# Decode attention and gated MLP with gradients on one core: layer norm on another engine, weight loads one turn earlier, a third PSUM pair at the end, a bf16 softmax shift

## The chip, the core and the metric

The kernel runs on one core of a Trainium2 chip. A core has five engines that run their own instruction streams, each in order: PE (TensorE, matrix products; its weight loads are listed apart as PEld), DVE (VectorE), ACT (ScalarE), POOL (GpSimd) and SP (SyncE). They work out of SBUF (128 partitions), PE writes into PSUM (8 banks of 128 x 512 fp32), and 16 DMA engines move data between SBUF and HBM. In this kernel SP issues nearly all loads and POOL nearly all stores. The metric is the device time of one execution in microseconds, the median over runs. Lower is better.

## What is computed

A forward pass and all its gradients, for batch 2 and a single query position, with bf16 data:

```python
xn = layernorm(x)                                   # x: 2 x 1 x 576
q  = xn @ wq                                        # 32 heads of 128
k, v = caches of 16 heads x 4096 x 128, each for 2 query heads
p  = softmax(q . k * 128 ** -0.5)
A  = (p . v) @ wo
B  = ((xn @ w_gate) * (xn @ w_up)) @ w_down         # 576 -> 4608 -> 576
out = x + A + B
# outputs: out, and for a given grad_out the gradients of
# x, k_cache, v_cache, wq, wo, w_gate, w_up, w_down
```

The caches are 2 x 16 x 4096 x 128 (33.6 MB each) and are read once; their gradients, as large, are written once. With the weights and their gradients 92.5 MB are read and 92.5 MB written.

## The kernel before, in words

**Attention.** The main loop has 16 steps (`NIT`): four groups of four KV heads, two batch rows, two halves of two heads. A step loads two K heads and two V heads, 1 MB each (`head_load`). `slot` handles one head: in two halves, `head_scores` transposes 128 x 1024 elements on DVE (`t32`, into `X`) and multiplies them on PE into a PSUM tile of the tag "sc" (two buffers). After the two K heads comes `softmax`: the maximum per partition (`mx`), a PE transpose to one row (`mT`), a maximum over the row (`m4`), its repetition (`mr`), a one-row product that spreads it over the partitions (`nb_ps`), then the exponential on ACT and the sums. All of this up to the exponential is fp32. After the V heads come `dscores` and `end_of_V`; `end_of_K` of a step follows early in the next step. Each of these two contains a `contract` of 64 matmuls over the heads' tiles, after which the tiles' buffers are free. Loads of heads and weights share one tag of 12 buffers, "nat", so a load is issued on SP only when an earlier tile is done with.

**Gradients of the caches.** They are outer products of one row with another. `outer_units` returns eight units for each step and cache: a unit makes 8 matmuls into a PSUM pair (`ps_o`, 128 x 2 x 512 fp32, two buffers), and `evac` copies it to SBUF as bf16, on DVE or ACT, whichever has the smaller running load (`load["v"]`, `load["s"]`). Four units fill 1 MB, which POOL then stores. The SBUF staging tiles of all stores share a tag, "st", of five buffers.

**Side work.** The MLP is cut in nine slices of 512 columns. `mlp_units` gives eight lists of functions for a slice: `loads` (wgu, wd: 1.77 MB), then `gate_up` and `down`, `grads` and `back`, and five lists of outer products with evictions. `back_units` gives nine lists for a finished group of heads: `first` (the output product with wo, the transposes `R`, and the stationaries `Wm` on DVE and `Wt` on POOL), `second` (the gradient of the norm through `dxn`), then the gradients of wo (`outer_o`, staged in `sto`) and wq (`outer_q`, `outer_qt`, staged in `stq` and `stqt`). The lists wait in `side`. In every slot, `more(2)` issues two units of cache gradients after each half, and then `other(per)` issues the next `per` lists, where `per` is a quarter of what is waiting. A new slice is added when fewer than five lists wait.

**The end.** After the loop: `end_of_K`, the K gradients of the last step, the last group's `back_units`, mixed with `final_units` (`prepare`, `output`: the forward result; `rows`: a product over `accx` on PE that gathers the gradient of the norm; `gradient`: nine small DVE steps over 2 x 576 elements and a store).

**The start.** The layer norm is eight DVE instructions over 2 x 576 elements with one square root on ACT (lines 168 to 188). POOL meanwhile clears the tiles `Wdy`, `W` (two), `dM` and others. DVE then prepares small constant tiles from the identity matrix, the last being `sel2`.

**Order.** A scheduler lays out each engine's instructions by priority and by its own estimates, and each engine then runs its stream strictly in that order, waiting on semaphores. `Block` keeps a unit's matmuls together.

Of the kernel before, what the change touches and what calls it, by code (L numbers as in the profile page):

```python
# [23 lines left out]
def kernel(  # L24
# [57 lines left out]

    class Block:
# [20 lines left out]
    def evac(out, in_, cols):  # L104
        cv = 0.16 + cols * 0.00104
        cs = 0.19 + cols * 0.00083
        if load["v"] + cv < load["s"] + cs:
            load["v"] += cv
            nc.vector.tensor_copy(out=out, in_=in_)  # L109
        else:  # L110
            load["s"] += cs
            nc.scalar.copy(out, in_)  # L112

# [43 lines left out]
    for be in range(4):  # L157
        nc.vector.tensor_copy(sel[:, be], view(ident[:], 0, P, 64 * (be // 2) + be % 2, [[0, 4], [2, 32]]))
        nc.vector.tensor_copy(selA[:, be], view(ident[:], 0, P, 32 * be, [[0, 4], [1, 32]]))
    one1 = const.tile([1, 1], FP32, name="one1")  # L160
# [7 lines left out]
    nc.vector.tensor_copy(x_f[:], x_bf[:])  # L168

    mu = const.tile([2, 1], FP32, name="mu")  # L170
    nc.vector.reduce_sum(mu[:], x_f[:], axis=AX.X)
    nc.vector.tensor_scalar(mu[:], mu[:], 1.0 / D, None, op0=ALU.mult)
    xn_f = sb.tile([2, D], FP32, tag="nat", bufs=12, name="xn_f")
    nc.vector.tensor_scalar(xn_f[:], x_f[:], mu[:], None, op0=ALU.subtract)
    xsq = sb.tile([2, D], FP32, tag="X", bufs=3, name="xsq")
    var = const.tile([2, 1], FP32, name="var")
    nc.vector.tensor_tensor_reduce(
        out=xsq[:], in0=xn_f[:], in1=xn_f[:], scale=1.0 / D, scalar=0.0,
        op0=ALU.mult, op1=ALU.add, accum_out=var[:],
    )  # L180
# [3 lines left out]
    nc.scalar.activation(rstd[:], var[:], AF.Sqrt, bias=eps_t[:], scale=1.0)  # L184
    nc.vector.reciprocal(rstd[:], rstd[:])
    nc.vector.tensor_scalar(xn_f[:], xn_f[:], rstd[:], None, op0=ALU.mult)
    xn_bf = sb.tile([2, D], BF16, tag="st", bufs=5, name="xn_bf")
    nc.vector.tensor_copy(xn_bf[:], xn_f[:])
# [27 lines left out]
    nc.gpsimd.memset(Wdy[:], 0.0)  # L216
# [8 lines left out]
    for t in range(2):  # L225
        nc.gpsimd.memset(W[t][:], 0.0)
    nc.gpsimd.memset(dM[:], 0.0)
# [340 lines left out]
    def outer_units(rows, bd, b, l0, oview):  # L568
        m = {}

        def unit(x, ch, A):
            def f():
                if ch == 0 and A == 0:
                    m["st"] = stile([P, 4, 8, Dh], "so")
                st = m["st"]
                o = ps_o()
                with Block() as mm:
                    for c in range(4):
                        for aa in range(2):
                            a = 2 * A + aa  # L580
                            mm(o[:, aa, c * Dh:(c + 1) * Dh], lhsT=rows[32 * a:32 * a + 32, 4 * ch + c, :],
                                             rhs=bd[32 * a:32 * a + 32, x * Dh:(x + 1) * Dh], start=True, stop=True)
                evac(st[:, 2 * A:2 * A + 2, 4 * ch:4 * ch + 4, :].rearrange("p a c d -> p a (c d)"), o[:], 1024)
                if ch == 1 and A == 1:
                    nc.gpsimd.dma_start(oview[b, :, :, l0 + x].rearrange("a m n -> m a n"),  # L585
                                        st[:].rearrange("p a c d -> p a (c d)"))
            return f
        return [unit(x, ch, A) for x in range(2) for ch in range(2) for A in range(2)]

    def softmax(s_ps):  # L590
        mx = small("mx")
        nc.vector.reduce_max(mx[:], s_ps[:], axis=AX.X)
        mT = ps_m([1, P])
        nc.tensor.transpose(mT[:], mx[:], identf[:])
        m4 = small("m4", (1, 4))
        nc.vector.reduce_max(m4[:], mT[0:1, :].rearrange("o (a m) -> o m a", m=4), axis=AX.X)
        mr = small("mr", (1, 32, 4), FP32, 1)
        nc.vector.tensor_copy(mr[:], view(m4[:], 0, 1, 0, [[0, 32], [1, 4]]))
        nb_ps = ps_m([P, 1])
        nc.tensor.matmul(nb_ps[:], lhsT=mr[:].rearrange("o a m -> o (a m)"), rhs=one1[:], start=True, stop=True)  # L600
        negb = small("negb")
        nc.vector.tensor_scalar(negb[:], nb_ps[:], -SCALE, None, op0=ALU.mult)
        ex = small("ex", (P, P), FP32)
        z = small("z")
        nc.scalar.activation(ex[:], s_ps[:], AF.Exp, bias=negb[:], scale=SCALE, accum_out=z[:])
        z_ps = ps_m([P, 1])
        nc.tensor.matmul(z_ps[:], lhsT=G4[:].rearrange("p a m -> p (a m)"), rhs=z[:], start=True, stop=True)
        rz = small("rz")
        nc.vector.reciprocal(rz[:], z_ps[:])

        pr = small("pr", (P, P), BF16)
        nc.vector.tensor_scalar(pr[:].rearrange("p (j c) -> p j c", c=4), view(ex[:], 0, P, 0, [[1, 32], [32, 4]]),  # L612
                                rz[:], None, op0=ALU.mult)
        pT = rowT[0][n_rows[0] % 2]
        n_rows[0] += 1
        t32(pT[:, 0:P], view(pr[:], 0, P, 0, [[1, 4], [4, 32]]))
        dve(0.3 + 0.3 + 0.3 + 0.2 + 0.2 + 0.25 + 0.25)
        act(0.5)
        return pr, pT, ex, rz
# [21 lines left out]
    def back_units(st):  # L641
        g, wq, wo, oT = st["g"], st["wq"], st["wo"], st["oT"]
        n0 = g * GH * Dh
        m = {}

        def first():
# [6 lines left out]
            nc.vector.tensor_add(acc[:], acc[:], yp[:])  # L653

            rp = ps_m([P, 2, 2, P], BF16)
            for t in range(2):
                for h in range(GH):
                    a = h // 2
                    nc.tensor.transpose(rp[32 * a:32 * a + 32, t, h % 2, :], oT[:, t, h, :], ident[:])
            m["R"] = R = sb.tile([P, 2, 2, P], BF16, tag="R", bufs=1, name="R")  # L660
            nc.vector.tensor_copy(R[:], rp[:])
# [6 lines left out]
            dve(0.2 + 0.5)  # L668
# [4 lines left out]
        def outer_q(k, A):  # L673
            def f():
                R = m["R"]
                if A == 0:
                    m["st"] = swtile([P, 2, GH * P], "stq")
                st = m["st"]
                o = ps_o()
                with Block() as mm:  # L680
                    for dc in range(2):
                        for aa in range(2):
                            a = 2 * A + aa
                            d0 = (2 * k + dc) * P
                            mm(o[:, aa, 256 * dc:256 * dc + 256], lhsT=xnr[32 * a:32 * a + 32, d0:d0 + P],
                                             rhs=R[32 * a:32 * a + 32, 1].rearrange("p h d -> p (h d)"),
                                             start=True, stop=True)
                evac(view(st[:], 0, P, 512 * A, [[256, 2], [GH * P, 2], [1, 256]]),
                     o[:].rearrange("p a (d n) -> p a d n", d=2), 1024)
# [18 lines left out]
        def outer_o(A, h2, k):  # L708
            def f():
                R = m["R"]  # L710
                if h2 == 0 and k == 0:
                    m["so"] = swtile([P, 4, D], "sto")
                o = ps_o()
                with Block() as mm:
                    for aa in range(2):
                        a = 2 * A + aa
                        mm(o[:, aa, 0:HD2], lhsT=R[32 * a:32 * a + 32, 0, h2, :],
                                         rhs=dyr[32 * a:32 * a + 32, k * HD2:(k + 1) * HD2], start=True, stop=True)
                evac(view(m["so"][:], 0, P, h2 * D + k * HD2, [[2 * D, 2], [1, HD2]]), o[:, :, 0:HD2], D)
# [5 lines left out]
        return [[first], [second], [outer_o(0, 0, 0), outer_o(0, 0, 1)], [outer_o(0, 1, 0), outer_o(0, 1, 1)],  # L725
# [10 lines left out]

    def other(n):
        for _ in range(min(n, len(side))):
            for f in side.pop(0):
                f()  # L740

# [103 lines left out]
    for n in range(NIT):  # L845
# [5 lines left out]
        per = max(1, -(-len(side) // 4))  # L851
# [33 lines left out]
        if new:  # L885
            st = nxt
    end_of_K(*last[:5])
    outs += outer_units(last[5], last[6], last[1], G * last[0]["g"] + 2 * last[2], okview)
    units = back_units(last[0])
    side += final[:1] + units[:2] + final[1:] + units[2:]  # L890
# [33 lines left out]
```

## Time and profile before

| | us |
|---|---|
| median of 13 runs | 521.16 |
| lowest, highest run | 515.25, 528.97 |
| the profiled execution, whole | 518.26 |
| its span, first to last instruction | 516.5 |
| PE busy, of the span | 421.5 (82%) |
| DVE busy | 356.5 (69%) |
| ACT busy | 328.1 (64%) |
| POOL busy | 206.2 (40%) |

The page of one profiled execution gives the busy time of each engine, the span in 40 slices of 12.9 us with the TensorE clock that was granted (tenths of full speed) and the DMA engines' share and rate, the chain of work that ended last, and groups of instructions with the mean duration of one. Idle time of an engine counts only where that engine is what others wait for. The prediction quotes the slices and stretches of time, single instructions in order of time at the start and at the end, and waits. In rows of instructions the first two numbers are start and duration in us; in square brackets stands the idle time before it and what ended it.

The DMA engines moved 186.26 MB, 361 GB/s over the span. Most stores are `so` tiles, 64 of 1 MB. The evictions that fill them, `so<-ps_o`, are 232 on ACT at 1022 ns and 24 on DVE at 1194 ns.

### The profile page before, as it was taken

Reading aid. Unit: us, or ns where it says so; the run is one execution under the profiler, and the core shown is the slowest. Engines: PE = TensorE matmul, PEld = TensorE weight load, DVE = VectorE, ACT = ScalarE, POOL = GpSimd, SP = SyncE. Lnnn points to the kernel's source line nnn. Section 1 sums busy time; section 2 is a strip of 40 time slices with the busy share of each in tenths; the row PEclk is TensorE's granted clock in tenths of the full one; section 3 lists DMA queues with packets and bytes.
Section 4 is the critical chain, followed back from the end, with each engine's and each line's share of the span. In section 5 each row is a group of like instructions: output and inputs, shape, how many; then the busy total and the mean of one; then the engine's idle time right before and its main releaser. Section 6 shows DMA issues by size and latency. Waiting matters only on the chain.

```text
span 516.5 us, 20063 instructions
## 1 busy us (share of the span) xinstructions
PE 421.5 (82%) x8921; PEld 337.3 (65%) x8921; DVE 356.5 (69%) x624; ACT 328.1 (64%) x454; POOL 206.2 (40%) x372
## 2 busy tenths in 40 slices
PE   1677987888888988988999889878988968899872
PEld 0576765776776666776777767666777757777630
DVE  7687866368667948376676688748685659598464
ACT  1234887658676465667587765758767565788653
POOL 6133353332642444333433434446243155453313
PEclk9989999579997767677858986989888699899655
DMA  8997999999999999898998999999999998976656
GB/s 256 405 390 294 390 400 386 396 411 402 342 389 388 360 359 414 303 404 320 387 404 312 412 418 398 378 412 402 403 404 367 418 384 346 378 278 236 248 193 235
DMA packets 52911, 186.26 MB, mean 361 GB/s; under 512 B 4140, under 2 KB 19128, under 8 KB 44632
## 3 DMA queue, kind: packets, MB, share of 16 engines
q1 hardware_dynamic: 28392, 92.49, 47.7%
q0 software_dynamic: 24432, 92.48, 45.2%
q8 instruction: 70, 1.15, 0.9%
q14 instruction: 17, 0.14, 0.1%
HBM read 92.48 MB, written 92.48 MB: 358 GB/s over the span
## 4 chain that ended last, share of the span: by engine, by line
PE 42%; DVE 16%; ACT 15%; DMA 14%; issue 8%; POOL 3%; POOLq 0%; DVEq 0%; ACTq 0%
PE ps_sc L93 16%; ACT so L112 12%; PE ps_o L93 11%; PE ps_m L93 10%; DVE X L121 5%; DMA out_dram<-so 3%; DMA wgu<-in_B_w_gate_dram 3%; DMA kv<-in_A_k_cache_dram 3%; DVE so L109 2%; DMA out_dram<-std 2%; DVE Xw L121 2%; DMA kv<-in_A_v_cache_dram 2%; PE ps_m L558 1%; DMA out_dram<-stqt 1%; POOL prm L564 1%
## 5 line engine op out<-in xcount | busy, mean ns | idle before, releaser
L112 ACT CAST so<-ps_o 128x1024 bf16<-128x1024 f32 x232 | 225.3, 1022 | 64.8 <-PE ps_o L93 58.6
L121 DVE STREAM_TRANSPOSE X<-kv 128x1024 f32<-128x1024 f32 x128 | 157.5, 1233 | 56.2 <-PE ps_sc L93 50.5
L93 PE MATMUL ps_sc<-X,W 128*128 128x128 bf16 x2048 | 164.1, 240 | 14.3 <-issue 7.7
L93 PEld LDWEIGHTS <-W 128*128 128x128 bf16 x2048 | 145.8, 108 | 22.5 <-issue 16.4
L585 POOL DMA_DIRECT2D out_dram<-so x64 | 49.9, 779 | 124.8 <-ACT so L112 78.1
L93 PE MATMUL ps_o<-bd,dsm 32*128 32x128 bf16 x1024 | 48.8, 240 | 13.4 <-ACT so L112 8.2
L93 PE MATMUL ps_o<-bd,prm 32*128 32x128 bf16 x1024 | 45.0, 231 | 12.4 <-ACT so L112 4.6
L93 PEld LDWEIGHTS <-dsm 32*128 32x128 bf16 x1024 | 29.7, 102 | 28.3 <-issue 22.6
L93 PE MATMUL ps_m<-kv,rowT 128*32 128x128 bf16 x2048 | 42.3, 244 | 5.3 <-issue 4.5
L93 PEld LDWEIGHTS <-prm 32*128 32x128 bf16 x1024 | 27.3, 98 | 24.9 <-issue 18.0
L93 PEld LDWEIGHTS <-rowT 128*32 128x32 bf16 x2048 | 35.3, 109 | 8.3 <-issue 6.0
L112 ACT CAST stw<-ps_o 128x1024 bf16<-128x1024 f32 x28 | 28.0, 1020 | 17.9 <-PE ps_o L93 16.6
L496 POOL COPY W<-rep 32x16 bf16<-32x16 bf16 x128 | 24.9, 195 | 28.5 <-PE ps_sc L93 21.2
L564 POOL TENSOR_TENSOR prm<-pr,maskc 128x1024 bf16<-128x1024 bf16 x16 | 30.2, 1890 | 13.6 <-DVE pr L612 13.4
L564 POOL TENSOR_TENSOR dsm<-ds,maskc 128x1024 bf16<-128x1024 bf16 x16 | 30.3, 1894 | 9.2 <-DVE ds L632 8.7
L109 DVE CAST so<-ps_o 128x1024 bf16<-128x1024 f32 x24 | 28.7, 1194 | 3.3 <-PE ps_o L93 3.3
L396 POOL DMA_DIRECT2D out_dram<-stw x18 | 13.7, 759 | 32.1 <-ACT stw L112 16.7
L121 DVE STREAM_TRANSPOSE Xw<-wgu 128x1152 f32<-128x1152 f32 x18 | 24.5, 1361 | 1.9 <-PE ps_sc L93 1.8
L503 POOL COPY dM<-qd 128x128 bf16<-128x128 bf16 x32 | 9.2, 291 | 41.5 <-PE ps_m L509 27.8
L112 ACT CAST sto<-ps_o 128x576 bf16<-128x576 f32 x25 | 15.1, 643 | 16.8 <-PE ps_o L93 16.8
L112 ACT CAST std<-ps_o 128x576 bf16<-128x576 f32 x36 | 22.1, 648 | 5.3 <-PE ps_o L93 3.9
L93 PEld LDWEIGHTS <-xnr 32*128 32x128 bf16 (+1 forms) x440 | 13.6, 100 | 17.1 <-issue 12.2
(172 smaller groups left out, 556.1 us busy)
## 6 DMA issues: line engine op xcount, KB each, us to landing
out_dram<-so POOLq DMA_DIRECT2D x64, 1024.0 KB, 10.8
kv<-in_A_k_cache_dram SPq DMA_DIRECT2D x32, 1024.0 KB, 12.0
kv<-in_A_v_cache_dram SPq DMA_DIRECT2D x32, 1024.0 KB, 10.2
out_dram<-stw POOLq DMA_DIRECT2D x18, 512.0 KB, 9.8
wd<-in_B_w_down_dram SPq DMA_DIRECT2D x9, 576.0 KB, 10.0
out_dram<-std POOLq DMA_DIRECT2D x9, 576.0 KB, 8.2
wo<-in_A_wo_dram SPq DMA_DIRECT2D x4, 1152.0 KB, 14.1
wgu<-in_B_w_gate_dram SPq DMA_DIRECT2D x9, 512.0 KB, 20.5
```

What stands on the lines that cost most here:

```text
L93: ins = nc.tensor.matmul(*args, **kwargs)
L109: nc.vector.tensor_copy(out=out, in_=in_)
L112: nc.scalar.copy(out, in_)
L121: nc.vector.transpose(out, in_)
L396: nc.gpsimd.dma_start(out[0:512, f0:f0 + FS].rearrange("(c p) n -> p c n", p=P), st[:])
L496: nc.gpsimd.tensor_copy(view(W[t][:], 32 * a, 32, 28 + 32 * a, [[2 * WW, 4], [WW + 2, 2], [1, 2]]), view(st["rep"][:], 32 * a, 32, t * 4 * ...
L503: nc.gpsimd.tensor_copy(view(dM[:], 0, P, t * 2 * P, [[P + 2, 2], [4, 32], [1, 2]]), view(st["qd"][:], 0, P, (2 if t == 0 else 1) * GH * 2 ...
L558: nc.tensor.matmul(t_ps[:], lhsT=o_sb[:], rhs=RV[:].rearrange("p x r -> p (x r)"), start=True, stop=True)
L564: nc.gpsimd.tensor_tensor(m[:], view(rows[:], 0, P, 0, [[0, 8], [1, P]]), view(maskc[:], 0, P, 0, [[1, 8], [0, P]]), ALU.mult)
L585: nc.gpsimd.dma_start(oview[b, :, :, l0 + x].rearrange("a m n -> m a n"), st[:].rearrange("p a c d -> p a (c d)"))
```

## The change

1. **Start.** x_f with its sum, xn_f, the square with its sum, and xn_bf are made on ACT. DVE keeps the one-element steps (`negmu`, `mu`, the reciprocal). The clearing of `Wdy`, `dM` and one `W` moves from POOL to DVE.
2. **Softmax shift.** `mx`, `mT`, `m4`, `mr` and the constant `one1` are bf16, and the transpose uses the bf16 identity.
3. **Side work in the loop.** `other` returns after it has issued a slice's `loads`, and its next call does nothing. `per` is a third of the waiting lists, not a quarter.
4. **`back_units`.** `first` is split into `output`, `turn(0)`, `turn(1)` and `spread`, in two lists; `output` and `turn(0)` need V's result alone. The last group stages `stq` and `sto` in "nat" buffers.
5. **The end.** Once `ending` is set, every third pair that `ps_pair` hands out is made of two single banks of the tag "sc", and `evac_pair` empties such a pair in two halves. The load counters are set to zero, and some of the side lists come before the last `end_of_K`.

```diff
+    def ps_pair():
+        pairs_made[0] += 1
+        if ending and pairs_made[0] % 3 == 0:
+            o = [ps.tile([P, 512], FP32, tag="sc", bufs=2, name="ps_x") for _ in range(2)]
+            return [t[:] for t in o], None
+        o = ps_o()
+        return [o[:, 0, :], o[:, 1, :]], o
+    def evac_pair(out, o, whole, cols, view_in=lambda t: t):
+        if whole is not None:
+            evac(out(None), view_in(whole[:]), cols)
+        else:
+            for a in range(2):
+                evac(out(a), view_in(o[a]), cols // 2)
...
-    one1 = const.tile([1, 1], FP32, name="one1")
+    one1 = const.tile([1, 1], BF16, name="one1")
...
-    nc.vector.tensor_copy(x_f[:], x_bf[:])
-    nc.vector.reduce_sum(mu[:], x_f[:], axis=AX.X)
+    nc.scalar.activation(x_f[:], x_bf[:], AF.Copy, accum_out=mu[:])
+    nc.vector.tensor_scalar(negmu[:], mu[:], -1.0 / D, None, op0=ALU.mult)
...
-    nc.vector.tensor_scalar(xn_f[:], x_f[:], mu[:], None, op0=ALU.subtract)
+    nc.scalar.activation(xn_f[:], x_f[:], AF.Identity, bias=negmu[:], scale=1.0)
...
-    nc.vector.tensor_tensor_reduce(
-        out=xsq[:], in0=xn_f[:], in1=xn_f[:], scale=1.0 / D, scalar=0.0,
-        op0=ALU.mult, op1=ALU.add, accum_out=var[:],
-    )
+    nc.scalar.activation(xsq[:], xn_f[:], AF.Square, accum_out=var[:])
...
-    nc.scalar.activation(rstd[:], var[:], AF.Sqrt, bias=eps_t[:], scale=1.0)
+    nc.scalar.activation(rstd[:], var[:], AF.Sqrt, bias=eps_t[:], scale=1.0 / D)
     nc.vector.reciprocal(rstd[:], rstd[:])
-    nc.vector.tensor_scalar(xn_f[:], xn_f[:], rstd[:], None, op0=ALU.mult)
-    nc.vector.tensor_copy(xn_bf[:], xn_f[:])
+    nc.scalar.activation(xn_bf[:], xn_f[:], AF.Copy, scale=rstd[:])
...
-    nc.gpsimd.memset(Wdy[:], 0.0)
+    nc.vector.memset(Wdy[:], 0.0)
...
-    for t in range(2):
-        nc.gpsimd.memset(W[t][:], 0.0)
-    nc.gpsimd.memset(dM[:], 0.0)
+    nc.vector.memset(dM[:], 0.0)
+    nc.vector.memset(W[0][:], 0.0)
+    nc.gpsimd.memset(W[1][:], 0.0)
...
-        mx = small("mx")
+        mx = small("mx", (P, 1), BF16)
         nc.vector.reduce_max(mx[:], s_ps[:], axis=AX.X)
-        mT = ps_m([1, P])
-        nc.tensor.transpose(mT[:], mx[:], identf[:])
-        m4 = small("m4", (1, 4))
+        mT = ps_m([1, P], BF16)
+        nc.tensor.transpose(mT[:], mx[:], ident[:])
+        m4 = small("m4", (1, 4), BF16)
...
-        mr = small("mr", (1, 32, 4), FP32, 1)
+        mr = small("mr", (1, 32, 4), BF16, 1)
...
-        return [[first], [second], [outer_o(0, 0, 0), outer_o(0, 0, 1)], ...
+        return [[output, lambda: turn(0)], [lambda: turn(1), spread], [second], [outer_o(0, 0, 0), outer_o(0, 0, 1)], ...
...
     def other(n):
+        if waits[0]:
+            waits[0] -= 1
+            return
         for _ in range(min(n, len(side))):
-            for f in side.pop(0):
+            group = side.pop(0)
+            for f in group:
                 f()
+            if group[0].__name__ == "loads":
+                waits[0] = 1
+                return
...
-        per = max(1, -(-len(side) // 4))
+        per = max(1, -(-len(side) // 3))
...
+    ending.append(1)
+    load["v"] = load["s"] = 0.0
+    waits[0] = 0
+    units = back_units(last[0])
+    side += final[:1] + units[:1] + final[1:2] + units[3:5]
+    more(2)
     end_of_K(*last[:5])
     outs += outer_units(last[5], last[6], last[1], G * last[0]["g"] + 2 * last[2], okview)
-    units = back_units(last[0])
-    side += final[:1] + units[:2] + final[1:] + units[2:]
+    side += units[1:3] + final[2:] + units[5:]
     while outs or side:
         more(2)
         other(1)
```

`outer_units`, `outer_q` and `outer_o` take their pairs from `ps_pair` and empty them through `evac_pair`; `outer_qt`, the MLP's units and `final_units` still use `ps_o` and `evac`.

## The prediction, made before the changed kernel ran

> **What bounds it now.** I read the slices of the page first, then the table by stretches, then the order of time at both ends, and last the waits.
>
> ```profile
> PEclk9989999579997767677858986989888699899655
> DMA  8997999999999999898998999999999998976656
> GB/s 256 405 390 294 390 400 386 396 411 402 342 389 388 360 359 414 303 404 320 387 404 312 412 418 398 378 412 402 403 404 367 418 384 346 378 278 236 248 193 235
> ...
> 45.00:50.00 5.00, 3.93 (x167) 3.17 (x168) 2.21 (x6) 2.93 (x5) 3.74 (x2) 1.00 0.54 175
> 205.00:210.00 5.00, 5.00 (x101) 3.93 (x98) 2.39 (x6) 3.35 (x6) 3.67 (x2) 0.50 0.77 306
> 460.00:480.00 20.00, 18.48 (x446) 14.76 (x447) 17.05 (x27) 17.94 (x25) 8.39 (x8) 1.00 0.67 251
> 480.00:500.00 20.00, 15.96 (x297) 9.83 (x286) 9.56 (x20) 10.79 (x13) 4.20 (x7) 0.56 0.60 225
> 500.00:516.50 16.50, 5.78 (x36) 1.48 (x35) 9.22 (x15) 5.91 (x8) 4.96 (x7) 0.50 0.57 208
> 60.00:445.00 385.00, 331.60 (x7087) 269.04 (x7084) 262.06 (x446) 259.36 (x363) 158.99 (x282) 0.83 0.99 383
> ```
>
> (Columns: stretch, busy us and count of PE, PEld, DVE, ACT, POOL, TensorE clock, DMA share, GB/s.) Three stages. From 60 to 445 us the DMA engines are the bound, 0.99 busy; they run dry only where a load waits for a buffer (205-210 and its like; with the dry time at 42-50 us some 13 us by the 5 us stretches). From 460 us nothing is left to load and evictions set the pace: ACT 17.9 and DVE 17.1 of 20 us. From 480 us nobody is full and the clock is 0.50; PE, eviction and PE again take turns. The head:
>
> ```profile
> 0.74 1.28 ACT L184 ACT_TABLE_LOAD   x1 [0.74 <-PEq L908]
> 1.47 2.02 POOL L216 MEMSET Wdy<- 128x2304 bf16 x1
> 2.08 2.78 DVE L168 CAST x_f<-x_bf 2x576 f32<-2x576 bf16 x1 [0.95 <-DMA x_bf<-in_A_x_dram]
> 8.88 0.45 DVE L188 CAST xn_bf<-xn_f 2x576 bf16<-2x576 f32 x1
> 9.26 0.21 DVE L130 CAST identf<-ident 128x128 f32<-128x128 bf16 x1
> 11.52 0.18 DVE L192 COPY sel<-ident 2x128 bf16<-2x128 bf16 x1
> ```
>
> The constants that gate the first matmuls stand behind the norm on DVE. Whoever waits for weights, and the tail:
>
> ```profile
> DVE Xd L121 <- DMA wd<-in_B_w_down_dram: 7.2, 2, 3.9
> ...
> 185.06 1.09 PEld L93 LDWEIGHTS <-xs 128*32 128x32 bf16 x39 [0.20 <-DMA wgu<-in_B_w_gate_dram]
> ...
> 482.67 0.64 PE L93 MATMUL ps_o<-bd,prm 32*128 32x128 bf16 x16 [1.85 <-issue]
> 488.72 0.63 POOL L274 COPY Wt<-Wm 64x128 bf16<-64x128 bf16 x2 [2.42 <-DVE Wm L268]
> 495.98 2.29 PE L804 MATMUL ps_o<-accx,F 128*2 128x160 f32 x8 [0.35 <-ACT so L112]
> 511.96 0.56 POOL L706 DMA_DIRECT2D out_dram<-stqt  x1
> ```
>
> Weights are waited for 7.2 us in all, by DVE, and 0.2 us by PE, though the chain names their DMAs for longer. The last store is issued at 511.96; the span ends 4.5 us later.
>
> **The skill.** "GPSIMD Engine Reference", Specifications: POOL's SBUF interfaces are shared with VectorE and contend with DVE in a two-port mode. The trace agrees: the same 2x576 cast takes 2.78 us beside POOL's memset and 0.45 us (other direction) without. "ScalarE: Activation LUTs", What ACT_TABLE_LOAD costs: 1.28 us, and 1.38 us of drain at a switch of sets. The trace has the 1.28; no run shows the drain. "TensorE: Matmul & The Clock Gate", Part 1: the array falls to half clock when it has been idle and rises only after sustained work. The trace agrees with the first half (0.56, then 0.50); 205-210 us is PE busy 5.00 of 5 and still 0.50, so rising is not quick.
>
> **Part by part.** *Layer norm on ACT.* Six DVE steps over 2x576 go: 2.78, 0.74, 0.87, 0.75, 0.79, 0.45 us. ACT takes x_f, xn_f, the square and xn_bf. No 2x576 ACTIVATE is in the trace; 128x576 evictions are 0.64 us, the accumulator read is 0.19 (row at 473.11). The new order puts a second table load ahead of the square root. x lands at 2.03: x_f 0.64+0.19 to 2.9; DVE is then busy with the Wdy, dM and W memsets that came over from POOL (2,032 four-byte elements; accx's 160 took 0.19, so at most 2.4 us from 0.9, to 3.3); negmu 0.14 to 3.45; xn_f, 0.64+0.1, 4.2; square 0.83, 5.0; load 1.28, 6.3; root 0.29, reciprocal 0.15, with hand-overs 6.9. The DVE constants then start at 6.9, not 9.26: -2.4. With the drain it is -1.0; without a visible load -3.7. I take -2.4, since the only load measured is 1.28. What follows is not held by data: Xo's transposes ran back to back behind DVE work at 15.52, K's at 23.47. An earlier start frees the first buffers earlier and fills the dry time at 45-50 us (0.46 of 5 us, and 0.5 before it), so all of it counts: -2.4.
>
> *Softmax in bf16.* The fp32 transpose (0.29 us) and the two-pass product (2 x 0.26) of each of 16 steps become one bf16 pass each. Nothing shows a 1-row bf16 transpose; bounds 0 and half of 0.8 us, 16 times: 0 to -6.4. But DMA is the bound there, and PE waited for DVE's mr for 1.6 us in all. I take -0.8.
>
> *Weights ahead.* `other` returns after a slice's loads, skips a turn, and takes a third of the units at a time, not a quarter. What can go is the 7.2 us of DVE's waiting for wd, at 98.6-102.6 (DMA full) and 236-239 (dry after it). PE's wait is 0.2. Bounds 0 and -7.2; I take -1.5. On SP, the sixth slice's five loads (1.77 MB) move behind later K and V loads, so bytes are the same. Against it, units now come in two turns of three after two turns of none; in PE's new order runs of four and five eviction pairs stand where two or three stood. PE makes a pair in 0.40 us, ACT empties it in 1.02, both engines together in about 0.56, so a further pair in a run costs PE 0.15 to 0.6. Three more in each of nine slices: 4 to 16 us of PE, mostly beside a full DMA. I take +1, bounds 0 and +13.
>
> *The end.* A third pair of banks, emptied as two 512-column halves, load counters at zero, more units before the last K contraction. Against what it seems to promise I count the new order from the end of that contraction (480.83 now, the last store begun 31.1 us later, of it 1.85 a PE gap). PE at clock 0.5 now has 16 blocks at 0.55 (8.8; 14 before), RV 0.5, wo 1.06, turns 1.4, spread 0.2, Wm 1.0, acc 1.23, five of R's blocks 2.2: 16.4, and by going through the evictions one by one it waits about 2 for them. But POOL's two Wt copies now stand behind the last K store and the first sto store: an eviction 0.64, issue 0.75, Wt 0.63, then PE 0.24, accx 2x0.32, accx's product 2.29, rowf's rest 0.7, and the gradient's nine DVE steps (0.74, 0.74, 0.07, 0.14, 0.5, 0.63, 0.73, 0.5, 0.74: 4.8). Behind these on DVE are two stq evictions of 1.23, then stq 0.74 and stqt 0.55 on POOL. The sum to the beginning of the last store: 18.4+2.0+0.24+0.64+2.29+0.7+4.8+2.5+1.3 = 32.9. That is 1.7 later than now; the two blocks put off bring the contraction forward by 1.1 to 2.0. So 0, bounded by -4 (clock at 1.0: PE's 16.4 becomes about 10, then ACT's 13 us of evictions hold) and +4 (the gap comes again, and hand-overs). I take 0.
>
> Sum: -2.4-0.8-1.5+1+0 = -3.7. The profiled execution is 518.3 us (span 516.5 and 1.8 around it), so 514.6. It lies 2.9 below the median of the runs, 521.2; on that scale 517.5.
>
> **Rivals.** *No change:* the 2.4 us at the head are given back at the next wait for a buffer, as 60-445 us is 0.99 full. For it: any stretch after 50 us. Against: dry time once removed comes back only where another opens. -3.7+2.4 = -1.3: about 520. *A larger gain:* with a block always ready PE stays at full clock in the end (-4), and the dry times at 240-250 and 275-285 (some 4 us) close: -3.7-4-4 to about 509.5. For it 1.00 at 460-480 us; against, 205-210. *Slower, by bunching:* in the last two turns of each of nine iterations PE stands at evictions, the V scores behind it come late, and so do both contractions that free the buffers; the DMA then runs dry at each iteration's end as it does at 205-210. It decides from 0.8 us a slice on: 9 x 0.81 = 7.3 is the 4.7 of gains above without the +1, and 2.6 to pass the limit. At the upper 13 us: -3.7+12 = +8, about 529.5; I put it at 528. For it: PE is busy 332 of 385 us there, the least slack after DMA. Against: DMA share 0.99, and 12 buffers that even out an iteration. *That a part does nothing:* weights ahead, by the 0.2 us; it is in the sums.
>
> **Numbers.** Chances: small gain 0.33 (512 to 518.5), larger gain 0.13, no change 0.21 (518.6 to 523.8; 0.5%, what a measurement of this kernel can tell from no change), slower 0.33. So faster 0.46, same 0.21, slower 0.33; predicted 517.5. Cases of both signs hold the chance: the likeliest one's own range is 512 to 519; the range of all goes from 507 (the larger gain, and the 1.9 us of dry time at 205-215 with it: 507.6) to 529.5.
>
> **What would show it.** Head: xn_bf at about 7.5 us and the first wq matmul near 10.4, not 12.82; the 45-50 us stretch over 0.8. A 1.4 us gap after the second table load makes the head -1.0. Middle: Xd without waits for wd; PE's waits on evictions up and the DMA share of 60-445 us below 0.97 would make the rival right. End: Wt on POOL later than the last K store, the two stq evictions after dx_bf, the last store about 33 us behind the last contraction; a clock near 1.0 there would give the larger gain. The prediction is wrong if the dry times grow in the middle.

## The result, and the profile after

| | before | after |
|---|---|---|
| median of the runs, us | 521.08 | 535.03 |
| lowest, highest, us | 515.06, 528.97 | 525.98, 540.06 |
| profiled execution, whole / span, us | 518.26 / 516.5 | 540.06 / 537.6 |
| ratio after to before | | 1.0154, 95% interval 1.011 to 1.0198 |

The change makes the kernel about 1.5% slower by the ratio, some 8 us; the medians are 14 us apart. The ratio compares only the faster executions of each kernel (four of the changed one, 527.5 us on the mean), the medians take in the slower ones too, and the profiles of the changed kernel and of runs 1 and 12 below are of slower ones. Times late in the span of this profile thus read about 2% high, and below I use shares and order more than totals.

First the slices of the page of the changed kernel (clock in tenths, DMA share in tenths, GB/s), to be laid beside those before:

```profile
PEclk9889977786895569886959585977998867699855
DMA  8999999999699898997996989999996999976783
GB/s 249 406 381 379 419 397 394 386 359 369 213 401 323 283 419 290 402 408 293 399 383 232 415 287 401 387 386 386 350 409 225 417 417 410 329 291 260 266 305 132
```

Before, no slice from the second to the 32nd moved less than 294 GB/s. Now seven do: 213, 283, 290, 293, 232, 287 and 225. The stretches say the same (columns: stretch, busy us and count of PE, PEld, DVE, ACT, POOL, clock, DMA share, GB/s):

```profile
45.00:50.00 5.00, 4.51 (x83) 3.60 (x82) 2.67 (x3) 4.33 (x8) 1.55 (x4) 1.00 1.01 371
60.00:445.00 385.00, 319.90 (x6642) 260.47 (x6641) 246.81 (x420) 242.20 (x336) 145.30 (x259) 0.77 0.94 360
480.00:500.00 20.00, 18.08 (x482) 14.66 (x482) 17.73 (x33) 16.62 (x22) 8.28 (x8) 1.00 0.70 264
500.00:537.60 37.60, 23.56 (x377) 13.16 (x369) 19.78 (x37) 20.01 (x30) 11.50 (x16) 0.59 0.63 232
```

The dry time at 45 to 50 us is gone (1.01, was 0.54). But over 60 to 445 us the DMA share fell from 0.99 to 0.94 and the rate from 383 to 360 GB/s. 0.05 of 385 us is 19 us. The start, in order of time (start, duration, engine):

```profile
2.23 0.68 ACT L190 ACTIVATE x_f<-x_bf 2x576 f32<-2x576 bf16 x1 [0.21 <-DMA x_bf<-in_A_x_dram]
...
4.81 1.28 ACT L201 ACT_TABLE_LOAD   x1
...
6.11 0.29 ACT L201 ACTIVATE rstd<-var,eps_t 2x1 f32<-2x1 f32 x1
...
6.62 0.77 ACT L204 ACTIVATE xn_bf<-xn_f,rstd 2x576 bf16<-2x576 f32 x1 [0.22 <-DVE rstd L202]
...
10.07 1.22 PE L105 MATMUL ps_m<-xs,wq 128*128 128x2 bf16 x40
```

The last of these rows before the change:

```profile
12.82 1.22 PE L93 MATMUL ps_m<-xs,wq 128*128 128x2 bf16 x40
```

x_f takes 0.68 us on ACT, where the cast on DVE took 2.78. xn_bf is ready at 7.39 and the first product with wq starts at 10.07, 2.75 us earlier than before. How the loads run dry is seen at one stretch, 140 to 145 us (DMA share 0.11):

```profile
130.57 0.34 SPq L536 DMA_DIRECT2D kv<-in_A_k_cache_dram  x1
...
134.71 3.91 PE L105 MATMUL ps_m<-Xo,Wdy 128*128 128x128 bf16 x36
...
144.32 1.08 PE L105 MATMUL ps_m<-kv,rowT 128*32 128x128 bf16 x64
...
145.44 1.18 SPq L536 DMA_DIRECT2D kv<-in_A_v_cache_dram  x2
...
140.00:145.00 5.00, 3.36 (x112) 2.94 (x113) 4.22 (x9) 2.79 (x3) 2.77 (x11) 1.00 0.11 40
```

The same place before the change:

```profile
120.87 0.34 SPq L520 DMA_DIRECT2D kv<-in_A_k_cache_dram  x1
...
132.70 2.24 PE L93 MATMUL ps_m<-Xo,Wdy 128*128 128x128 bf16 x36
...
138.34 1.43 SPq L520 DMA_DIRECT2D kv<-in_A_v_cache_dram  x2
...
135.00:140.00 5.00, 3.19 (x114) 2.58 (x112) 3.00 (x9) 4.43 (x6) 2.83 (x5) 1.00 0.82 272
```

The contraction of V (64 products, `kv,rowT`) ends at 145.40, and only then SP issues the next V loads. No load was issued for 14.9 us. The product `Xo`, `Wdy` of the next group belongs to the main loop and stood ahead of the contraction before, too, and SP's pause there was longer, 17.5 us, with a DMA share no lower than 0.82. So a pause on SP alone does not make the DMA run dry; how much is still under way counts as well, and these rows do not tell that. The stretch shows where the loads are missing, not yet what the change did to them. The waits of SP in 60 to 450 us (line, who ended the wait, us in total, times, longest) show a second releaser:

```profile
SPq L536 <- DVE Xw L141: 18.9, 2, 11.7
SPq L335 <- DVE Xw L141: 12.5, 2, 6.3
```

The same rows before:

```profile
SPq L520 <- DVE Xw L121: 3.6, 1, 3.6
SPq L319 <- DVE Xw L121: 3.5, 1, 3.5
```

`Xw` is the last use of a slice's `wgu`: loads stood 31.4 us for weights that were not yet used up, where it was 7.1 before. The waits of DVE for loads moved from the weights to the caches. After the change no row has wd, and these two have the caches (before, the K row was 3.4 us and there was no V row):

```profile
DVE X L141 <- DMA kv<-in_A_k_cache_dram: 9.8, 3, 6.6
DVE X L141 <- DMA kv<-in_A_v_cache_dram: 3.8, 2, 2.4
```

So 7.2 us of waiting for wd went and 10.2 us of waiting for cache loads came. The end, in order of time:

```profile
519.83 0.65 POOL L290 COPY Wt<-Wm 64x128 bf16<-64x128 bf16 x2
...
528.37 0.75 DVE L870 TENSOR_TENSOR dx_bf<-t,dy_f 2x576 bf16<-2x576 f32 x1
529.04 2.34 DVE L121 CAST stq<-ps_o 128x1024 bf16<-128x1024 f32 x2
...
532.65 1.11 POOL L731 DMA_DIRECT2D out_dram<-stqt  x2
```

POOL's `Wt` copies come after the last K store, and the last two stq evictions on DVE after dx_bf. From the end of K's last contraction (502.06) to the beginning of the last store (the second of two from 532.65, about 533.2) it is 31.1 us, as before. In this execution the end neither gained nor lost; the middle lost.

### The profile page after: what moved, and what is told of

It reads as the page before. It is cut to its first block, busy times and chain, and to the rows that moved or that the text cites. A ratio compares the mean times of both kernels' runs of the same rounds, so it can differ in the third digit from the quotient of the medians.

```text
span 537.6 us, 20047 instructions
## 1 busy us (share of the span) xinstructions
PE 435.9 (81%) x8905; PEld 349.9 (65%) x8905; DVE 355.6 (66%) x628; ACT 333.9 (62%) x466; POOL 201.4 (37%) x369
## 4 chain that ended last, share of the span: by engine, by line
PE 42%; DVE 11%; ACT 9%; issue 7%; DMA 7%; POOL 1%; DVEq 0%; POOLq 0%; ACTq 0%
PE ps_sc L105 14%; PE ps_m L105 13%; PE ps_o L105 10%; ACT so L124 7%; DVE X L141 5%; DMA out_dram<-so 3%; DMA kv<-in_A_k_cache_dram 2%; DVE so L121 2%; PE ps_m L574 1%; DMA kv<-in_A_v_cache_dram 1%; DMA out_dram<-sto 1%; PE ps_m L625 1%; DVE Xw L141 1%; PE ps_m L525 1%; ACT sto L124 1%
## 5 line engine op out<-in xcount | busy, mean ns | idle before, releaser
L124 ACT CAST so<-ps_o 128x1024 bf16<-128x1024 f32 x228 | 221.0, 1020 | 67.7 <-PE ps_o L105 58.5
L105 PE MATMUL ps_o<-bd,prm 32*128 32x128 bf16 x1016 | 47.8, 235 | 12.8 <-ACT so L124 7.2
L105 PEld LDWEIGHTS <-dsm 32*128 32x128 bf16 x1024 | 31.8, 104 | 34.5 <-issue 29.4
L124 ACT CAST stw<-ps_o 128x1024 bf16<-128x1024 f32 x30 | 29.5, 1015 | 31.3 <-PE ps_o L105 22.6
L105 PEld LDWEIGHTS <-prm 32*128 32x128 bf16 x1024 | 29.5, 100 | 25.4 <-issue 18.9
L580 POOL TENSOR_TENSOR prm<-pr,maskc 128x1024 bf16<-128x1024 bf16 x16 | 30.3, 1892 | 14.7 <-DVE pr L630 14.5
L512 POOL COPY W<-rep 32x16 bf16<-32x16 bf16 x128 | 24.8, 194 | 23.4 <-PE ps_sc L105 15.7
L105 PEld LDWEIGHTS <-Wdy 128*128 128x128 bf16 x306 | 28.8, 133 | 5.3 <-DVE Xo L141 2.9
L124 ACT CAST std<-ps_o 128x576 bf16<-128x576 f32 x36 | 22.2, 646 | 14.5 <-issue 8.6
L571 ACT COPY o_sb<-ps_m 128x128 f32<-128x128 f32 x32 | 8.7, 271 | 26.8 <-PE ps_m L105 26.7
```

What stands on the lines that cost most here:

```text
L105: ins = nc.tensor.matmul(*args, **kwargs)
L512: nc.gpsimd.tensor_copy(view(W[t][:], 32 * a, 32, 28 + 32 * a, [[2 * WW, 4], [WW + 2, 2], [1, 2]]), view(st["rep"][:], 32 * a, 32, t * 4 * ...
L571: nc.scalar.copy(o_sb[:], o_ps[:])
L580: nc.gpsimd.tensor_tensor(m[:], view(rows[:], 0, P, 0, [[0, 8], [1, P]]), view(maskc[:], 0, P, 0, [[1, 8], [0, P]]), ALU.mult)
```

## The experiments

Three quantities from the traces are used beside the time. *Dry time* is what is missing to a full DMA in the 5 us stretches from 45 to 450 us (a stretch over 1.00 counts as full). *Hold* is the time for which a tile occupies one of the twelve shared "nat" buffers, from its load's issue on SP to its last use (weights: the later of `Xw` and the eviction of the gate product for wgu, of `Xd` and the step on `acc` for wd; cache tiles: the small DVE step behind their contraction), summed over the 18 tiles of the nine slices and over the 64 cache tiles. A hold is measured afterwards and grows with whatever delays a tile's users; run 13 is the one that lengthens it by itself. *Tail* is from the last `rowT<-ds` on DVE, the input of K's last contraction, to the end of the span. There is one profile for each kernel.

| kernel | ratio to before, 95% | dry, us | hold of weights, us | hold of cache tiles, us | last rowT<-ds, us | tail, us |
|---|---|---|---|---|---|---|
| before | 1 | 13.4 | 719 | 3384 | 478.6 | 37.9 |
| after | 1.0154 (1.011, 1.020) | 29.2 | 885 | 3409 | 499.3 | 38.3 |
| 1 after, old loop | 1.014 (1.009, 1.019) | 22.3 | 728 | 3461 | 490.0 | 38.5 |
| 2 before, new loop | 1.027 (1.021, 1.034) | 26.1 | 901 | 3385 | 497.6 | 35.0 |
| 3 before, head and softmax | 0.9875 (0.982, 0.993) | 13.4 | 699 | 3349 | 476.0 | 37.5 |
| 4 before, new end and split | 1.020 (1.013, 1.027) | 20.0 | 734 | 3400 | 484.4 | 40.5 |
| 5 before, split alone | 1.016 (1.009, 1.022) | 25.0 | 748 | 3445 | 492.5 | 38.5 |
| 6 as 4, lists whole in the loop | 1.009 (1.005, 1.013) | 20.8 | 747 | 3431 | 489.1 | 37.3 |
| 7 before, a third at a time | 1.006 (1.002, 1.009) | 21.5 | 664 | 3459 | 487.5 | 37.9 |
| 8 before, skipped turn | 1.036 (1.030, 1.043) | 31.2 | 824 | 3461 | 499.1 | 36.6 |
| 9 as 8, loads held back | 1.014 (1.007, 1.020) | 23.3 | 681 | 3529 | 486.0 | 36.4 |
| 10 before, loads one head ahead | 1.034 (1.026, 1.042) | 28.1 | 837 | 3401 | 495.2 | 36.3 |
| 11 3 and new end, old loop | 0.988 (0.980, 0.995) | 18.1 | 712 | 3378 | 479.7 | 34.4 |
| 12 as 11, end counted | 0.981 (0.974, 0.988) | 15.2 | 723 | 3398 | 480.1 | 32.3 |
| 13 before, late reader | 1.051 (1.044, 1.058) | 38.2 | 1013 | 3303 | 506.0 | 38.0 |
| 14 control of 13 | 1.003 (0.999, 1.008) | 14.7 | 734 | 3390 | 481.0 | 37.4 |
| 15 after, first whole in the loop | 1.016 (1.004, 1.028) | 23.4 | 868 | 3352 | 492.6 | 35.0 |
| 16 as 12, slice in one list | 0.986 (0.983, 0.990) | 14.5 | 634 | 3446 | 481.2 | 31.7 |

The tail moves by a few us, the last rowT<-ds by up to thirty, and the ratio goes roughly with the dry time. A lower TensorE clock is not needed for a loss: the mean clock of the profile is 0.835 before, and 0.834 and 0.847 in runs 8 and 10, which lose 3.6 and 3.4%. In the profile of the changed kernel it is 0.791, where it may add.

**Whole parts.** Theory A, the rival of the prediction: the loop's new issue bunches work ahead of V's contraction. Theory B: the earlier start or the bf16 order throws buffers out of step. Theory C: the end costs.

Run 1, the changed kernel with the old loop:

```diff
     def other(n):
-        if waits[0]:
-            waits[0] -= 1
-            return
         for _ in range(min(n, len(side))):
-            group = side.pop(0)
-            for f in group:
+            for f in side.pop(0):
                 f()
-            if group[0].__name__ == "loads":
-                waits[0] = 1
-                return
...
-        per = max(1, -(-len(side) // 3))
+        per = max(1, -(-len(side) // 4))
```

> The changed kernel with the side work issued as before (no skipped turn after a slice's loads, a quarter of the waiting lists at a time). Theory A, bunching: the loss of 8 us and the gain of the head's 2.7 us are both real, so the loop costs about 10 us; without it the time is 2 to 4 us below the kernel before, ratio 0.992 to 0.997, and the dry stretches of DMA near 140, 280 and 400 us are gone. Theory B, the earlier start or the bf16 order throws the buffers out of step: still 5 us or more slower than before, ratio 1.01 or more. Theory C, the new end costs: ratio 1.005 to 1.015 with the last V loads issued near 437 us as before.

Run 2 is the reverse: these lines of the change alone, in the kernel before.

> The kernel before with only the new issue of the side work (skipped turn, a third at a time). Theory A: 10 us slower, ratio 1.015 to 1.025, dry DMA stretches in the middle, last V loads issued 10 us or more after 438 us. Theory B and C: within 0.5% of before, the DMA share of 60 to 445 us still 0.97 or more.

Run 3: parts 1 and 2 of the change alone (layer norm, moved clearing, bf16 shift).

> The kernel before with only the layer norm on ACT, the moved clearing of tiles and the bf16 softmax shift. Theory A: 2 to 4 us faster, ratio 0.992 to 0.997, last V loads issued 2 to 4 us earlier than 438. Theory B: slower by 1% or more. Theory C: as theory A. If the head's gain is given back at the next buffer wait: within 0.3%.

Run 4: parts 4 and 5 of the change alone (`back_units` in ten lists, `ps_pair`, new order of the end).

> The kernel before with only the new end and the split of the finished group's work in the loop. Theory A: within 0.5%, from the end of the last contraction of K to the end of the span 35 to 37 us (35.7 before, 35.5 in the changed kernel). Theory C: slower by 1% or more, most of it after the last V load or around the three groups' ends in the loop. Theory B: within 0.5%.

Head and softmax gain 1.25%, more than A expected, so B falls. The loop alone costs 2.7%, a little above A's range. But without it, in run 1, 1.4% of loss is left, against A; the ratio lies in C's range, but the last V loads are issued at 454.4, not near 437. Run 4 costs 2.0%, though only 2.6 us of it lie in the tail: the last V loads were issued at 448.8, and at 437.8 before. A second cause sits in the loop.

**The two causes taken apart.** Run 5: only the split of `first`, in the kernel before.

```diff
-        return [[first], [second], ...
+        return [[output, lambda: turn(0)], [lambda: turn(1), spread], [second], ...
```

> The kernel before with the finished group's first list split in two (and its R in two PSUM tiles), in the loop and at the end; nothing else. Theory D: the longer list of side work in the loop shifts units by a turn and costs what the new end seemed to cost in the middle, 5 to 6 us: ratio 1.008 to 1.015, DMA dry near 245 us for 5 us or more. Theory E, the end's own order is what costs: within 0.5% of before.

Run 6: run 4 with the two lists joined for the groups that finish inside the loop.

```diff
+        front = [[output, lambda: turn(0)], [lambda: turn(1), spread]]
+        if g != NGRP - 1:
+            front = [front[0] + front[1]]
```

> The new end, with the two new lists issued as one for the three groups that finish inside the loop; only the last group has them apart. Theory D: the middle is as before (last contraction's input ready near 478 to 479 us), what is left is the end's 2 to 3 us: ratio 1.000 to 1.006. Theory E: still slower by 1.5% or more.

Runs 7 and 8: only the third at a time, and only the skipped turn.

```diff
# run 7
-        per = max(1, -(-len(side) // 4))
+        per = max(1, -(-len(side) // 3))
# run 8
+        if waits[0]:
+            waits[0] -= 1
+            return
...
+            if group[0].__name__ == "loads":
+                waits[0] = 1
+                return
```

> The kernel before with a third of the waiting lists at a time, and no skipped turn. Theory A, bunching by larger turns: slower by 1% or more, DMA dry for 20 us or more of 45 to 450 us (13.4 before). Theory F, the skipped turn alone makes the loss: within 0.5%.

> The kernel before with the skipped turn after a slice's loads, and a quarter at a time as before. Theory A: near nothing or a gain of 1 to 2 us, as DVE no longer waits for wd (7.2 us before). Theory F: slower by 1.5% or more, DMA dry for 20 us or more.

The split alone costs 1.6%, a little above D's range, with DMA at 0.51 and 0.01 in 250 to 260 us, where a group ends. Joined lists give part of it back: run 4 lost 2.0%, and run 6, with the lists joined, loses 0.9%, between the ranges of D and E. In run 6 `R` still takes two PSUM tiles and two DVE copies, which no run has alone. Why the split costs time in the loop is not shown. DVE's wait for wd is 12.4 us in run 5 and 7.2 before, but it is 13.0 in run 11 below, which loses nothing. In the loop's issue, thirds cost 0.6%, between the ranges of A and F; the skipped turn costs 3.6%, more than twice what all of the change costs. Both together (run 2) cost 2.7%, less than the skipped turn alone, which is not explained. Theory A in its plain form, work in larger heaps, does not explain the skipped turn.

**Place or hold.** In run 8 a slice's loads stand two turns ahead of their use. That gave theory G: weights occupy shared buffers longer, and cache loads wait for them.

Run 9 keeps every list of run 8 in its turn but issues the loads only when the skipped turn is over; run 10 leaves every list where it was before and issues a slice's loads one head earlier.

```diff
# run 9
             if group[0].__name__ == "loads":
+                held.append(group[0])
                 waits[0] = 1
                 return
...
+        while held:
+            held.pop(0)()
# run 10, at the end of a step
+        if len(side) < 5 and nslice < NFS:
+            ahead = mlp_units(nslice)
+            ahead[0][0]()
+            side += [[lambda: None]] + ahead[1:]
+            nslice += 1
```

> The kernel before with the skipped turn (which cost 3.6%), and a slice's loads held back until the skipped turn is over, so that every other list stays in the turn it has with the skip. Theory A, the place of the work: the late units stand between the V scores and V's contraction on PE, whatever the loads do: still 2.5% or more slower than before. Theory G, the loads ahead: a slice's weights lie in the shared buffers for two more turns before they are transposed, and later cache loads wait for them (the waits of SP for Xw, 39 us in the run with the skip alone and none in the kernel before, go): 1.5% or less slower.

> The kernel before with a slice's loads issued at the end of the step before, one head earlier, and all other lists in the turns they had. Theory A: within 0.5% of before, or 1 to 2 us faster as DVE's 7.2 us of waiting for wd shrink. Theory G: slower by 1% or more, with SP waiting for Xw.

Run 9 loses 1.4% and run 10 3.4%: about six tenths of the skipped turn's loss come from the loads, and the rest from the place of the work. One thing went against the expectation of run 9: SP's waits of cache loads that ended with Xw did not go (39.1 us; 39.4 in run 8; before they were 3.6, not none). The name at the end of a wait is thus a poor measure; the hold, 681 against 824 us, is the better one. Run 10 in order of time, from the K load that came behind the weights to the next V load:

```profile
92.46 3.71 SPq L520 DMA_DIRECT2D kv<-in_A_k_cache_dram  x1
...
107.23 1.25 DVE L121 STREAM_TRANSPOSE X<-kv 128x1024 f32<-128x1024 f32 x1 [11.40 <-DMA kv<-in_A_k_cache_dram]
...
109.06 0.59 PE L607 MATMUL ps_m<-z,G 128*128 128x1 f32 x2 [11.35 <-ACT ex L605]
...
113.44 1.90 PE L93 MATMUL ps_m<-kv,rowT 128*32 128x128 bf16 x64
...
115.38 1.64 SPq L520 DMA_DIRECT2D kv<-in_A_v_cache_dram  x2
```

Two stretches of it, from the table of stretches of run 10:

```profile
110.00:115.00 5.00, 5.00 (x94) 4.34 (x94) 2.93 (x8) 2.84 (x4) 3.65 (x7) 0.50 0.02 3
115.00:120.00 5.00, 5.00 (x116) 4.21 (x108) 1.42 (x2) 3.10 (x5) 0.75 (x1) 0.51 0.88 287
```

The second K head of this step is issued at 92.46, behind a slice and a group's weights. DVE waits 11.4 us for it (in the brackets), PE 11.35 us for the softmax behind it, V's contraction ends at 115.34, and meanwhile nothing is left to load: DMA 0.02.

In run 10 the order on SP changes too. Run 13 changes the hold and little else: two one-element steps for each slice read the weights once more, about a turn after their last use; run 14 is its control and reads a constant instead. SP issues the loads in the same order in both; on the other engines the scheduler put a few per cent of the instructions in another place.

```diff
                 if A == 1 and w == 0:
+                    junk = sb.tile([1, 2], BF16, tag="junk", bufs=2, name="junk")
+                    nc.vector.tensor_tensor(junk[:, 0:1], m["wgu"][0:1, 0, 0:1], st[0:1, 0, 0:1], ALU.mult)
+                    nc.vector.tensor_tensor(junk[:, 1:2], m["wd"][0:1, 0, 0:1], st[0:1, 0, 0:1], ALU.mult)
```

> The kernel before, in which 18 one-element DVE steps (of 1.5 us in all at 0.08 us each) read each slice's wgu and wd once more after its first stw eviction, about a turn after their last real use; orders are otherwise nearly the kernel before's. Theory G, weights that lie longer in the shared buffers hold up the cache loads: a slice's two tiles are held 5 to 15 us longer, some 90 to 270 tile-us in all, a twelfth of which is 8 to 22 us: 1% or more slower than its control. Theory A, only the place of the work counts: as its control.

> The control: the same 18 one-element DVE steps, which read a constant in place of wgu and wd. Both theories: within 0.7% of before.

Run 13 loses 5.1% and run 14 0.3%. The 18 steps themselves cost next to nothing; what they keep occupied costs 21 us (544.95 to 523.95, medians). The waits of SP in run 13 (60 to 450 us):

```profile
SPq L319 <- DVE junk L396: 31.4, 2, 16.9
...
SPq L524 <- DVE junk L396: 20.3, 1, 20.3
...
SPq L442 <- DVE junk L397: 9.4, 1, 9.4
...
SPq L524 <- DVE junk L397: 3.6, 3, 1.3
```

66.3 us of SP's waits end with one of the two extra reads, 64.7 in these rows and 1.6 in one more. DVE's waits for K loads, in run 13 and in the control:

```profile
DVE X L121 <- DMA kv<-in_A_k_cache_dram: 35.1, 8, 11.1
```

```profile
DVE X L121 <- DMA kv<-in_A_k_cache_dram: 1.3, 1, 1.3
```

Stretches of run 13, then of the control:

```profile
60.00:445.00 385.00, 317.23 (x6719) 258.39 (x6718) 246.89 (x437) 246.13 (x344) 146.15 (x261) 0.80 0.93 359
```

```profile
60.00:445.00 385.00, 334.80 (x7057) 271.11 (x7056) 265.74 (x463) 257.08 (x360) 159.06 (x284) 0.81 0.99 381
```

The kernels do the same work, at 0.93 against 0.99 of a full DMA. The weights are held 279 us longer than in the control; divided by the twelve buffers that is 23 us, and the last rowT<-ds comes 24.9 us later. For the new loop alone (run 2) the same division gives (901 - 719) / 12 = 15 us, against 19.0 us at the last rowT<-ds and 14 by the ratio; between runs 8 and 9 it gives 12 us, and the ratios differ by 12. It is a rough size: for run 10 it gives 10 us where 17 were lost, and in run 13 the cache tiles are held 87 us less than in the control, with which the 23 us would be 16.

**The end by itself, and how the losses add.** Run 11 is run 3 with the new end, and `first` whole for groups inside the loop; every engine has run 3's order until the tail:

```diff
-        return [[output, lambda: turn(0)], [lambda: turn(1), spread], [second], ...
+        front = [[first]] if g != NGRP - 1 else [[output, lambda: turn(0)], [lambda: turn(1), spread]]
+        return front + [[second], ...
```

Run 12 makes the last `Wt` on DVE and counts DVE's last steps in the load that picks the evicting engine:

```diff
# run 12
-            nc.gpsimd.tensor_copy(
+            (nc.vector if ending else nc.gpsimd).tensor_copy(
...
         def output():
+            dve(1.6)
         def rows():
+            dve(1.2)
         def gradient():
+            dve(4.8)
```

> Head and softmax of the changed kernel and its new end, but the loop and the three finished groups inside it exactly as before: up to the tail each engine has the order of the kernel with head and softmax alone (0.9875). So the end is seen alone. Prediction's step, the end costs nothing: 0.983 to 0.992. If the new end costs 1%: 0.995 to 1.0. If it gains: below 0.98. From the last dscores on, 37.5 us in the kernel with head and softmax alone; POOL's copies of Wt stand earlier here than in the changed kernel, after the second of five stores, so 33 to 37.

> The same with the last Wt copies on DVE and the final steps of DVE (1.2 us of rows, 4.8 of gradient, 1.6 of output) counted in the load that picks the engine of an eviction, so that ACT takes the last stq evictions. If the tail hangs on Wt and on the stq evictions behind the gradient, as the prediction had it, 1 to 4 us below the other kernel of this call: 0.975 to 0.985, from the last dscores on 31 to 35 us. Else the same time.

The new end is worth nothing that can be measured in the ratio (0.988 beside 0.9875), though the tail of its one profile is 3.1 us shorter. Run 12 has the lowest ratio of all, 1.9% below the kernel before, with a median of 512.08 us. dx_bf is made there from 505.15 to 505.90. POOL's last steps in run 12, in order of time:

```profile
505.20 0.71 POOL L728 DMA_DIRECT2D out_dram<-stq  x1 [1.07 <-ACT stq L124]
507.10 0.72 POOL L728 DMA_DIRECT2D out_dram<-stq  x1 [1.19 <-ACT stq L124]
507.81 1.11 POOL L743 DMA_DIRECT2D out_dram<-stqt  x2
```

The first stq store is issued beside dx_bf; in the changed kernel the evictions of stq alone lasted 2.3 us after it. The intervals of runs 11 and 12 overlap, so that run 12 is the better of the two rests on the tail of one profile each (32.3 and 34.4).

Run 15: the changed kernel with run 11's edit, its new loop kept. Run 16: run 12 with a slice's inner lists joined.

```diff
# run 16
-        return [[loads], [gate_up, down], [grads, back], ...
+        return [[loads], [gate_up, down, grads, back], ...
```

> The changed kernel, with the finished group's first list whole again for the three groups inside the loop, and the new issue of the side work kept. Undoing the new issue alone gave 1.014, undoing both 0.9876. If the two losses add up, 1.6 and 2.7%: 0.995 to 1.003. If either one alone is enough to run the loads dry at the ends of groups: 1.008 to 1.02.

> The fastest kernel so far (0.981: head, softmax, the new end with DVE's last steps counted, loop as before) with gate_up, down, grads and back of a slice in one list, so that its weights are free about a turn earlier. Theory G: 18 tiles by 3 to 7 us earlier, a twelfth of it is 4 to 10 us: 0.965 to 0.978. Theory A: the lists are fewer and one turn is fuller, as with a third at a time (1.0056): 0.982 to 0.99.

Run 15 is as slow as the changed kernel (1.016, from few executions, with the widest interval of the table), and so was run 1 (1.014); only without both is it fast (run 11). Within these intervals either of the two takes the whole loss. Run 16 shortens the weights' hold by 89 us beside run 12 and lengthens that of the cache tiles by 48: (48 - 89) / 12 = -3 us by the division, and the measurement, 0.986 beside 0.981 with intervals that overlap, shows no gain. It lies in theory A's range. That a fuller turn makes the contractions late and so takes back what the shorter hold gave would fit, but is not shown.

## Why the prediction was wrong

*Layer norm on ACT, -2.4: right.* The second table load is 1.28 us and the square root starts 0.02 us behind it; the first product with wq is 2.75 us earlier, and 45 to 50 us went from 0.54 to 1.01. *Softmax, -0.8:* the fp32 product of two passes is one now. Together the two were put at -3.2; run 3 measures -1.25% of 521, -6.5 us with an interval of -9.3 to -3.7, while its profile shows only 3.0 less of span. By the interval they gained at least what was predicted; the runs do not tell the two apart.

*Weights ahead, -1.5 with +1 for bunching: this step failed.* DVE's wait for wd did go, from 7.2 us to nothing, and 10.2 us of waiting for cache loads came in its place. But the gain was bounded by 0 on one side, as if an earlier load could only help. No term stood for the buffers in which the weights lie meanwhile, although the text named the waits of loads for buffers as the reason for the dry times. "On SP, the sixth slice's five loads ... so bytes are the same" counted bytes, not occupied buffers. What the step has to say in its place: 182 us more hold of the weights (run 2), a twelfth of it 15 us, and 2.7%, 14 us, measured. The +1 for bunching was too small but inside its bounds of 0 and +13: a third at a time costs 0.6%, 3 us (run 7), and the place of the lists behind the skipped turn 1.4%, 7 us (run 9).

*The rival "slower, by bunching": the right place, half the cause.* Its signs came: PE's wait for ACT's evictions of `so` rose from 20.2 to 24.7 us, and the DMA share of 60 to 445 us is 0.94, below its 0.97. What bunching costs without longer holds of the weights is seen in runs 7 and 9 (0.6 and 1.4%, 3 and 7 us). The same wait of PE before, in run 7 and in run 9:

```profile
PE ps_o L93 <- ACT so L112: 20.2, 47, 1.2
```

```profile
PE ps_o L93 <- ACT so L112: 22.4, 46, 1.8
```

```profile
PE ps_o L93 <- ACT so L112: 29.3, 62, 2.3
```

It rose by 2.2 and 9.1 us, which fits the rival's mechanism, PE standing at evictions so that V's contraction is late; no run changes this wait alone. The larger part of the skipped turn's loss, 3.6% against 1.4%, is the hold, which no case of the prediction had. The rival got 0.33 with 528 us; the ratio puts the changed kernel at 1.0154 x 521 = 529, near it, but partly for another reason than the rival's.

*The end, 0: right for the end, but incomplete; here a second step failed.* It was 31.1 us where 32.9 were worked out, in the order that was worked out (`Wt` behind the last K store, stq behind the gradient). But the split of `first` was priced for the last group alone. The three groups that finish inside the loop get ten lists too, and there it costs 1.6% by itself (run 5), about 8 us. No term stood for it, and why it costs that stays open.

*The sum.* -6.5 (run 3) + 14 (run 2) + 8 (run 5) + 0 would be +16; measured is +8. The two losses do not add up (runs 1 and 15). That both lengthen the same dry stretches at the ends of groups would explain it, but was not tested. By subtraction (runs 4 and 6) about 1.1% of the split is the second list and the rest, if the end is nothing, the two-tile `R`; no run has that alone.

## What to carry to other kernels

Where loads wait for buffers of a shared pool, a tile's price is the time from its load's issue to its last use: sum that over the tiles a change touches and divide by the number of buffers before counting any gain from an earlier load. Here that gave the size within a few us in three cases of four. A load put further ahead of its use lengthens that time. In this kernel, whose DMA was 0.99 full, it paid in none of runs 2, 8 and 10; they lost 2.7 to 3.6%, runs 2 and 8 partly for the place of the lists. When a list of work is split or moved at the end, look for every other place that uses the same list.

## What the runs showed of the hardware that was not expected

The switch of table sets on ACT shows no drain: the step before ends at 4.79, the load runs from 4.81 to 6.09 and the next activation starts at 6.11. The Trainium skill, "ScalarE: Activation LUTs", What ACT_TABLE_LOAD costs, has 1.38 us of drain; the measurement decides.

TensorE stayed at half clock for a while though it was busy all the time, as at 205 us before: in run 10, after a pause of 11 us, PE is busy 5.00 of 5 us from 110 to 115 us at 0.50 and from 115 to 120 us at 0.51; from 120 us on the clock is 1.00.

Where a kernel runs dry differs between profiles. Runs 3 and 11 have the same order on every engine up to the tail, and yet their last rowT<-ds are at 476.0 and 479.7, with a DMA share of 0.83 and of 0.19 in 140 to 145 us. Their dry times are 13.4 and 18.1 us. The dry times of one profile are thus good to some 5 us, and the ratio of many executions has to decide.
